# Ten weight tiles get their exponent from GpSimd: a fused attention and MoE kernel on one core

## The chip, the core and the metric

The kernel runs on one core of one Trainium2 chip. The metric is the device time of one execution in microseconds (us); lower is better. PE is TensorE, DVE is VectorE, ACT is ScalarE, POOL is GpSimd, and SP is the engine whose queue issues most of the DMAs.

## What is computed

The input is q, k and v of 4 batches, 8 heads, 768 positions and 64 columns per head, in float32, with two numbers `n_global` (8) and `n_local` (96), and two weight matrices in float64: `w_in` (512 x 2048) and `w_out` (2048 x 512). The reference, cut to what matters:

```
scores = q k^T / sqrt(D) - slope_h * dist          # kept where key < n_global, or 0 <= rel < n_local
a = softmax(scores)
x = (a v)                                          # 3072 tokens x 512
h = x @ w_in
g = h * tanh(softplus(h))
out = g @ w_out
```

## The kernel before

The 3072 tokens are cut into 12 chunks of 256. Each chunk runs through attention in 8 pieces of two heads, and then through the MoE part in 8 steps of two blocks of 128 hidden columns each. For most products an operand is kept as the sum of two float16 halves, high and low, and a product takes three matmuls (high-high, high-low, low-high). The first three chunks have their attention in float32.

The weights come as float64, and there are 32 raw tiles of 128 x 512 float64 numbers: even tiles are columns of `w_in`, odd ones are rows of `w_out`. Every raw tile is loaded once by DMA and turned into its two float16 halves within the first 140 us, while the attention of the first chunks runs beside it. For one tile i the steps are these, each with the letter that the order list has for it:

- `w`, line 330: the DMA from SP's queue. The raw words of tiles 0 to 23 lie in the buffer `wts` in which finished halves are written later, so a half can only be written when the raw tile beneath it has been read.
- `A`, `exponent_w`, line 345: the upper 32-bit word of each number, read as a float32 with a stride of 8 bytes, is multiplied by 2^-111, and goes to a buffer `wc` (four of them) as float32. A multiplication by a power of two shifts the exponent field. An apostrophe behind the letter means that DVE does it (line 146), no apostrophe that ACT does it (line 148).
- `S`, `sign_w` (line 363 on DVE, line 365 on ACT), and `B`, `bits_w` (line 369, DVE): sign and low bits into a buffer `ws`.
- `C`, `join_w` (line 373, DVE): `wc` shifted and joined with `ws`. It reads two SBUF tensors and needs `A`.
- `D`, `high_w` (line 146 or 148): the high float16 half into `wts`.
- `E`, `low_w` (line 152): the low half, on POOL without an apostrophe, on DVE with one.

PE reads the halves in `moe_in` (token `i`, line 597; step m uses tiles 4(m mod 8) and 4(m mod 8) + 2) and in `moe_out` (token `o`, line 654; tiles 4(m mod 8) + 1 and + 3). One `moe_in` step is 24 matmuls, the first 12 for the first of its two tiles; in each group of three the first two read the high half and the third reads the low one.

The order of the work is written by hand in the string `PROGRAM` (line 737): every token issues the instructions of its step, and each engine works through its own instructions in the order in which the tokens stand. An engine that waits at one instruction holds back all that stand behind it. The tokens of the ten tiles lie in the first part of the list, from `A2'` to `A11`. POOL has, before the change, the low halves of weights (`E`), of attention weights (`p`, `d`) and of the MoE product (`Z`), always through the helper `rest` at line 152. DVE's helper is `copy` at line 146, where it is also used for tiles other than `wc`.

Of the kernel before, what the change touches and what calls it, by code (L numbers as in the profile page):

```python
# [12 lines left out]
F32 = mybir.dt.float32  # L13
# [3 lines left out]
ALU = mybir.AluOpType  # L17
# [18 lines left out]
EXPO = 2.0 ** -111  # L36
# [6 lines left out]
def tile_kernel(ctx, tc, qd, kd, qT, kT, v, n, w_in, w_out, out):  # L43
# [29 lines left out]
    with ExitStack() as st:  # L73
        windowed(st, tc, locals())
# [36 lines left out]
def windowed(st, tc, loc):  # L111


    nc = tc.nc
# [12 lines left out]
    STEP = P + NGMAX  # L127

    CF32 = 3
    WB = 4  # L130
    HELD = range(2 * NFP, 2 * NFP + 6)

# [10 lines left out]
    def copy(out, in_, scale, other=False):  # L143

        if other:
            nc.vector.tensor_scalar(out, in_, scale, None, op0=ALU.mult)  # L146
        else:
            nc.scalar.activation(out, in_, AF.Copy, scale=scale)  # L148
# [35 lines left out]
    def first_key(G):  # L184
        return OWN if (G // 2) % NCHB == 0 else 0

    def high_q(G, other=False):

        both = mt.tile([P, DM], I32, name="ws", bufs=WB).bitcast(F16).rearrange("p (x a c) -> p x a c", x=2, c=CH)
        split[G, "q"] = both[:, 0], both[:, 1]  # L190
# [6 lines left out]
    def high_k(G, other=False):  # L197
        o = first_key(G)
        split[G, "k"] = tuple(mt.tile([P, DM], F32, name="wc", bufs=WB).bitcast(F16)[:, 0:GH // 2 * KW].rearrange("p (a w) -> p a w", w=KW) for x in range(2))
        copy(split[G, "k"][0][:, :, o:], raw[G][1][:, :, o:], 1.0, other)  # L200
# [6 lines left out]
    def load_v(ci):  # L207
        if ci >= NC:
            return
        b, c = divmod(ci, NCHB)  # L210
        if ci < CF32:
            vr = vown[ci] = stk.tile([P, 2, DM], F32, name="vo")
# [16 lines left out]
    def window_v(ci):  # L229
        b, c = divmod(ci, NCHB)  # L230
        vc = stk.tile([P, 2, DM], F32, name="vc")
        if ci < CF32:
            far = L.v[b, 0:NGMAX, :]
# [76 lines left out]
    def begin(n):  # L310

        if not fills:
            fills.append(mt.tile([P, DM], I32, name="ws", bufs=WB).bitcast(F16)[:, 0:DM])
            nc.vector.memset(fills[0], 1.0)
# [30 lines left out]
    def exponent_w(i, other=False):  # L345

        r = wraw[i]
        c = mt.tile([P, DM], F32, name="wc", bufs=WB)
        copy(c, r[:, :, 1].bitcast(F32), EXPO, other)
        wst[i, 0] = c  # L350

    def words(i, w):
        if (i, 1) not in wst:
            wst[i, 1] = mt.tile([P, DM], I32, name="ws", bufs=WB)
        return wst[i, 1].bitcast(U16).rearrange("p (f w) -> p f w", w=2)[:, :, w]
# [62 lines left out]
    def scores(t):  # L418
# [5 lines left out]
        rows_ = slice(blk * P, (blk + 1) * P)  # L424
        if ci < CF32:
            qr, kr = raw[2 * ci + g]
# [13 lines left out]
    def largest(t):  # L440
# [7 lines left out]
        for j in range(2):  # L448
            h = g * GH + 2 * a2 + j
            m = mb0[:, h, :] if first else mb[:, h, :]  # L450
            nc.vector.tensor_tensor_reduce(out=A[:, j, 0:w], in0=sc[j][:, 0:w], in1=m, scale=-1.0 / (UNIT if ci < CF32 else UNIT * SQ), scalar=3.0e38, op0=ALU.add, op1=ALU.min, accum_out=nm[:, h:h + 1])  # L451
        pend[t] = A
# [46 lines left out]
    def weigh(t):  # L499
# [5 lines left out]
        vs = [vown[ci][:, blk]] if nk == 1 else [vcmp[ci][:, blk], vown[ci][:, blk]]  # L505
        if ci < CF32:
            pair = slice((g * GH // 2 + a2) * P, (g * GH // 2 + a2 + 1) * P)
# [16 lines left out]
    def rows(n):  # L524
# [4 lines left out]
        nc.vector.reciprocal(ri, rs)  # L529
        if ci < CF32:  # L530
            xhls[n] = ri
# [169 lines left out]
    def checks(i):  # L701
# [29 lines left out]
        "I": identity, "P": turn_p, "F": turned, "O": spread, "m": times_rb,  # L731
        "R": rows, "T": high_x, "U": low_x, "V": turn_x,
        "A": exponent_w, "S": sign_w, "B": bits_w, "C": join_w, "D": high_w, "E": low_w,
        "i": moe_in, "J": hold_h, "j": exp_h, "u": square_e, "n": ln_u, "r": inverse_u, "G": times_h, "H": times_r,
        "z": high_g, "Z": low_g, "o": moe_out, "Q": evacuate, "Y": store, "f": lambda i: flags(), "k": checks,
# [218 lines left out]
```

## Time and profile before

| what | value |
|---|---|
| runs | 605.38, 607.1 and 608.1 us, median 607.1 |
| profiled execution: span from the first to the last instruction | 602.9 us |
| profiled execution: its own time | not given apart; the median run is 4.2 us above the span |
| PE busy | 593.3 us, 98% |
| PEld (weight loads) busy | 407.6 us, 68% |
| DVE busy | 438.3 us, 73% |
| ACT busy | 454.0 us, 75% |
| POOL busy | 150.8 us, 25% |
| granted TensorE clock, mean | 0.998 |

The span is what the trace covers, and the time of a run holds what lies around it too. Busy shares are means over the whole span; the stages differ, so a share is to be read by stretch. A matmul's end is modelled in the profile, so the starts of matmuls are the better sign of whether PE goes on without a stop.

### The profile page before, as it was taken

How to read it: one execution, taken by the hardware profiler on the slowest of the kernel's cores; microseconds unless marked ns; L12 is line 12 of the kernel's file. 1: busy time of each engine (PE TensorE's matmuls, PEld its weight loads, DVE VectorE, ACT ScalarE, POOL GpSimd, SP SyncE). 2: the span in 40 equal slices, each digit the busy share in tenths (PEclk: the TensorE clock that was granted, in tenths of full speed). 3: DMA queues.
4: the chain of work that ended last, by engine and by line, in shares of the span. 5: the costliest groups of instructions: out<-in, count | busy, mean ns of one | idle time of the engine just before them, and what ended most of it. 6: DMA issues, size and time to landing. Idle time of an engine off the chain costs nothing.

```text
span 602.9 us, 14805 instructions
## 1 busy us (share of the span) xinstructions
PE 593.3 (98%) x5686; PEld 407.6 (68%) x5686; DVE 438.3 (73%) x1188; ACT 454.0 (75%) x1129; POOL 150.8 (25%) x128
## 2 busy tenths in 40 slices
PE   7999999999999999999999999999999999999996
PEld 3778677775666767757767676667767766766673
DVE  7999998998977795684876767576787766462443
ACT  6999999989978777669676778677777864655552
POOL 0133411331131423213133422141242121301020
PEclk9999999999999999999999999999999999999999
DMA  8999655233393672653464562753445351310001
GB/s 210 288 289 333 218 140 179 69 106 80 64 213 79 112 165 68 130 133 79 90 143 104 125 136 77 175 118 80 93 70 131 69 121 36 88 36 1 35 1 38
DMA packets 123066, 71.12 MB, mean 118 GB/s; under 512 B 91600, under 2 KB 112848, under 8 KB 122992
## 3 DMA queue, kind: packets, MB, share of 16 engines
q1 hardware_dynamic: 122416, 69.81, 48.5%
q8 instruction: 45, 0.74, 0.5%
q10 hardware_dynamic: 576, 0.34, 0.3%
q14 instruction: 29, 0.24, 0.1%
HBM read 38.62 MB, written 6.29 MB: 74 GB/s over the span
## 4 chain that ended last, share of the span: by engine, by line
PE 96%; DMA 1%; ACT 1%; DVE 0%; issue 0%; SPq 0%; DVEq 0%
PE ph L597 41%; PE po L654 37%; PE sc L437 5%; PE pav L521 4%; PE pav L654 3%; PE pav L512 2%; PE po L490 1%; DMA AT<-hl 1%; PE ph L543 1%; PE ph L490 1%; PE ph L318 1%; ACT A L460 0%; ACT u L623 0%; DVE sc L416 0%; ACT e L615 0%
## 5 line engine op out<-in xcount | busy, mean ns | idle before, releaser
L597 PE MATMUL ph<-xT,wts 128*128 128x256 f16 x2304 | 263.6, 273 | 0.0
L597 PEld LDWEIGHTS <-wts 128*128 128x128 f16 x2304 | 223.2, 98 | 35.2 <-issue 0.2
L654 PE MATMUL po<-wts,gt 128*128 128x512 f16 (+1 forms) x1062 | 239.0, 378 | 0.0
L654 PEld LDWEIGHTS <-gt 128*128 128x128 f16 x1158 | 110.7, 98 | 122.2 <-issue 0.4
L615 ACT ACTIVATE e<-ph 128x512 f32<-128x512 f32 x90 | 53.2, 591 | 95.8 <-PE ph L597 95.6
L152 POOL TENSOR_TENSOR gt<-gf,gt 128x512 f16<-128x512 f32 x50 | 62.0, 1241 | 229.9 <-DVE gt L146 155.7
L635 DVE CUSTOM_DVE_ANT_0 gf<-gf,u 128x512 f32<-128x512 f32 x96 | 72.4, 757 | 49.8 <-ACT u L627 48.0
L631 DVE SCALAR_TENSOR_TENSOR gf<-e,ph 128x512 f32<-128x512 f32 x90 | 61.0, 683 | 48.9 <-ACT e L615 47.9
L460 ACT ACTIVATE A<-A,nm 128x232 f32<-128x232 f32 (+1 forms) x192 | 88.2, 461 | 10.2 <-DVE nm L451 9.8
L152 POOL TENSOR_TENSOR hl<-A,hl 128x512 f16<-128x512 f32 (+1 forms) x43 | 50.6, 1186 | 110.2 <-ACT hl L148 56.8
L451 DVE CUSTOM_DVE_ANT_0 A<-sc,mb 128x232 f32<-128x232 f32 (+1 forms) x192 | 63.7, 375 | 13.1 <-PE sc L437 12.9
L627 ACT ACTIVATE u<-u 128x512 f32<-128x512 f32 x96 | 59.7, 625 | 1.9
L619 ACT ACTIVATE u<-e 128x512 f32<-128x512 f32 x96 | 59.8, 624 | 1.7
L623 ACT ACTIVATE u<-u 128x512 f32<-128x512 f32 x96 | 59.7, 623 | 1.7
L152 POOL TENSOR_TENSOR wts<-ws,wts 128x512 f16<-128x512 f32 x18 | 22.4, 1254 | 80.0 <-ACT wts L148 73.3
L152 DVE TENSOR_TENSOR gt<-gf,gt 128x512 f16<-128x512 f32 x46 | 34.3, 748 | 6.9 <-ACT gt L148 6.3
L460 ACT ACTIVATION_READ_ACCUMULATOR A<-A,nm 128x1 f32 x192 | 36.2, 188 | 0.0
L521 PEld LDWEIGHTS <-AT 128*128 128x128 f16 (+1 forms) x792 | 29.3, 97 | 8.2 <-DMA AT<-hl 2.0
L148 ACT ACTIVATE gt<-gf 128x512 f16<-128x512 f32 x39 | 24.3, 624 | 11.3 <-DVE gmax L635 9.2
L521 PE MATMUL pav<-vo,AT 128*128 128x64 f16 x432 | 28.0, 192 | 0.0
L146 DVE TENSOR_SCALAR gt<-gf 128x512 f16<-128x512 f32 x57 | 25.6, 453 | 1.5
L373 DVE SCALAR_TENSOR_TENSOR ws<-wc,ws 128x512 int32<-128x512 int32 x32 | 26.0, 832 | 0.2
(129 smaller groups left out, 559.7 us busy)
## 6 DMA issues: line engine op xcount, KB each, us to landing
wts<-w_in SPq DMA_DIRECT2D x12, 512.0 KB, 8.1
wts<-w_out SPq DMA_DIRECT2D x12, 512.0 KB
qr<-qT SPq DMA_DIRECT2D x23, 256.0 KB, 3.1
kr<-kd SPq DMA_DIRECT2D x32, 184.0 KB, 5.2
out<-ob SPq DMA_DIRECT2D x11, 512.0 KB
vr<-v SPq DMA_DIRECT2D x9, 512.0 KB
vc<-vo SPq DMA_DIRECT2D x15, 192.0 KB, 5.3
wr<-w_in SPq DMA_DIRECT2D x4, 512.0 KB, 7.8
```

The lines of the kernel that those rows point to most:

```text
L152: (nc.vector if other else nc.gpsimd).tensor_tensor(out, in_, high, op=ALU.subtract)
L451: nc.vector.tensor_tensor_reduce(out=A[:, j, 0:w], in0=sc[j][:, 0:w], in1=m, scale=-1.0 / (UNIT if ci < CF32 else UNIT * SQ), scalar=3.0e3 ...
L460: nc.scalar.activation(A[:, j], A[:, j], AF.Exp, bias=nm[:, h:h + 1], scale=-1.0, accum_out=rs[:, h:h + 1])
L521: nc.tensor.matmul(pav[:, cols], AT[rows_, (x * 2 + j) * nk + kk, :], vs[kk][rows_, y, cols], start=(n == 0), stop=(n == last))
L597: nc.tensor.matmul(ph[:, j, :].rearrange("p (b t) -> p b t", b=2), wv4[:, 2 * fb, x, c * P:(c + 1) * P], xT[:, :, y * NCC + c, :], start=( ...
L615: nc.scalar.activation(mish[m]["e"], mish[m]["h"], AF.Exp, scale=-1.0 / (SV * SW), accum_out=esum[:, m:m + 1])
L619: nc.scalar.activation(u, mish[m]["e"], AF.Square, bias=0.5)
L623: nc.scalar.activation(mish[m]["r"], mish[m]["u"], AF.Ln, bias=0.25 / RS, scale=1.0 / RS)
L627: nc.scalar.activation(r, r, AF.Exp, scale=-1.0)
L631: nc.vector.scalar_tensor_tensor(gf, mish[m]["e"], 0.5, mish[m]["h"], op0=ALU.add, op1=ALU.mult)
L635: nc.vector.tensor_tensor_reduce(out=gf, in0=gf, in1=mish[m]["r"], scale=SG / (SV * SW * RS), scalar=0.0, op0=ALU.mult, op1=ALU.max, accum ...
L654: nc.tensor.matmul(pos[ci][t][:, cols], gt[:, x, j, t * P:(t + 1) * P], wv4[:, 2 * fb + 1, y, cols], start=(fb == 0 and n == 0), stop=(fb ...
```

## The change

For the tiles 1, 2, 3, 4, 6, 7, 8, 10, 11 and 12 step `A` becomes one GpSimd instruction, whatever the token's apostrophe says. Before, tiles 2, 3, 4, 6 and 8 had it on DVE, and 1, 7, 10, 11 and 12 on ACT. The order list keeps its tokens and their order; POOL now meets the ten instructions at the places of these tokens, among its subtractions. All other tiles stay as they were, tiles 0 and 5 too.

```
+    POOLED = (1, 2, 3, 4, 7, 6, 12, 11, 10, 8)
...
         c = mt.tile([P, DM], F32, name="wc", bufs=WB)
-        copy(c, r[:, :, 1].bitcast(F32), EXPO, other)
+        if i in POOLED:
+            nc.gpsimd.tensor_scalar(c, r[:, :, 1].bitcast(F32), EXPO, None, op0=ALU.mult)
+        else:
+            copy(c, r[:, :, 1].bitcast(F32), EXPO, other)
         wst[i, 0] = c
```

## Rows read from the trace of the kernel before

**Rows 1.** The page: busy us, share of the span and instructions of each engine.

```profile
PE 593.3 (98%) x5686; PEld 407.6 (68%) x5686; DVE 438.3 (73%) x1188; ACT 454.0 (75%) x1129; POOL 150.8 (25%) x128
```

**Rows 2.** Busy time by stretch: stretch, length, each engine, PEclk, DMA share, GB/s.

```profile
14.80:56.00 41.20, 41.20 (x505) 31.51 (x506) 39.29 (x146) 40.51 (x119) 9.43 (x8) 1.00 1.06 307
56.00:140.00 84.00, 84.00 (x714) 61.60 (x715) 78.94 (x171) 78.24 (x166) 26.51 (x20) 1.00 0.52 150
140.00:385.80 245.80, 245.80 (x2467) 165.19 (x2465) 182.53 (x490) 188.65 (x482) 67.30 (x55) 1.00 0.52 112
```

**Rows 3.** Waits of PE: who waited for whom, us, times, longest.

```profile
PE ph L318 <- DVE ws L314: 2.7, 1, 2.7
PE pav L521 <- DMA AT<-hl: 0.9, 1, 0.9
```

**Rows 4.** Instructions at tile wc, 0 to 60 us: ns min/median/max, starts, forms.

```profile
L373 DVE SCALAR_TENSOR_TENSOR ws<-wc,ws x11: 641/687/931, 17.1 to 56.0; 128x512 int32<-128x512 int32 x11
L146 DVE TENSOR_SCALAR wc<-wts x7: 409/420/431, 15.6 to 51.0; 128x512 f32<-128x512 f32 x7
L148 ACT ACTIVATE wc<-wts x5: 669/677/682, 27.2 to 55.0; 128x512 f32<-128x512 f32 x5
```

**Rows 5.** Timeline of DVE, 47 to 54 us: start, us, instruction, idle before.

```profile
47.84 0.41 DVE L146 TENSOR_SCALAR wc<-wts 128x512 f32<-128x512 f32 x1
48.17 0.39 DVE L451 CUSTOM_DVE_ANT_0 A<-sc,mb 128x232 f32<-128x232 f32 x1
...
50.10 0.64 DVE L373 SCALAR_TENSOR_TENSOR ws<-wc,ws 128x512 int32<-128x512 int32 x1
...
51.97 0.69 DVE L631 SCALAR_TENSOR_TENSOR gf<-e,ph 128x512 f32<-128x512 f32 x1 [0.56 <-ACT e L615]
...
53.26 0.68 DVE L152 TENSOR_TENSOR wts<-ws,wts 128x512 f16<-128x512 f32 x1
```

**Rows 6.** POOL's groups by form, 0 to 60 us: busy us, mean ns, idle before.

```profile
L152 POOL TENSOR_TENSOR wts<-ws,wts 128x512 f16<-128x512 f32 x9 | 10.8, 1215 | 43.6 <-ACT wts L148 40.5 <-DVE rs L527 3.1
...
L261 POOL IOTA u<- 128x128 f32 x1 | 0.2, 238 | 0.0
...
L262 POOL IOTA e<- 128x96 f32 x1 | 0.2, 211 | 0.0
```

**Rows 7.** Timeline of POOL, 18 to 72 us.

```profile
18.81 1.17 POOL L152 TENSOR_TENSOR wts<-ws,wts 128x512 f16<-128x512 f32 x1 [17.37 <-ACT wts L148]
29.26 1.16 POOL L152 TENSOR_TENSOR wts<-ws,wts 128x512 f16<-128x512 f32 x1 [9.28 <-ACT wts L148]
...
48.33 1.16 POOL L152 TENSOR_TENSOR wts<-ws,wts 128x512 f16<-128x512 f32 x1 [2.29 <-ACT wts L148]
56.29 2.55 POOL L152 TENSOR_TENSOR wts<-ws,wts 128x512 f16<-128x512 f32 x2 [6.80 <-ACT wts L148]
...
69.03 1.16 POOL L152 TENSOR_TENSOR gt<-gf,gt 128x512 f16<-128x512 f32 x1 [3.57 <-issue]
70.16 1.60 POOL L152 TENSOR_TENSOR wts<-ws,wts 128x512 f16<-128x512 f32 x1
```

**Rows 8.** Timeline of DVE, 20 to 47 us.

```profile
22.36 0.46 DVE L369 TENSOR_SCALAR ws<-wts 128x512 uint16<-128x512 uint16 x1 [0.28 <-DMA wts<-w_in]
...
27.55 0.69 DVE L373 SCALAR_TENSOR_TENSOR ws<-wc,ws 128x512 int32<-128x512 int32 x1
```

**Rows 9.** Timeline of PE, 26 to 34 and 47 to 57 us.

```profile
29.75 2.78 PE L597 MATMUL ph<-xT,wts 128*128 128x256 f16 x24
...
53.21 2.78 PE L597 MATMUL ph<-xT,wts 128*128 128x256 f16 x24
```

**Rows 10.** Timeline of SP's DMA issues, 5 to 40 us.

```profile
27.00 0.29 SPq L239 DMA_DIRECT2D vc<-v  x1
```

**Rows 11.** The chain that ended last, in order of time: start, us, what.

```profile
53.37 2.62 PE ph L597 x24
```

**Rows 12.** Timeline of DVE, 68 to 78 us.

```profile
69.09 1.65 DVE L373 SCALAR_TENSOR_TENSOR ws<-wc,ws 128x512 int32<-128x512 int32 x1
```

## The prediction

> **What bounds the kernel now.** I read the page's engine totals first: TensorE (PE) is busy 593.3 of 602.9 us [rows 1]. A busy PE need not be one at its peak, so the next view was the busy time by stretch, cut where PE's behaviour changes: 14.8 to 56 us holds the ten tiles of the change, and PE is busy for all 41.20 us of it, as for the whole of the two stretches behind it, 84.00 and 245.80 us [rows 2]. Third came PE's waits [rows 3]: 2.7 us on the very first matmul, before any weight is read, and 0.9 us on one transposed attention tile in the last part. PE thus runs without a visible gap from 14.8 to 385.8 us. The granted clock is 1.00 in all three stretches, its level of 2.4 GHz [rows 2], so the sum has no term for the clock.
>
> The other side of the same table matters as much: in 14.8 to 56 us VectorE (DVE) is busy 39.29 and ScalarE (ACT) 40.51 of 41.20 us, GpSimd (POOL) only 9.43 [rows 2]. The change moves work from the two full engines to the idle one. But those two do not make PE wait there: whatever they save can shorten the end only by removing PE time, and there is none to remove.
>
> **What the change removes.** Each of five ACT copies (tiles 1, 7, 12, 10, 11) takes 677 ns in the median, each of five DVE copies (2, 3, 4, 6, 8) 420 ns [rows 4]; on DVE the next instruction starts 0.33 us after such a copy's start (47.84 to 48.17) [rows 5]. So ACT gets back 5 x 0.68 = 3.4 us and DVE 5 x 0.33 = 1.65 us. On the end both are worth 0, since PE covers them; were that cover gone they would be worth at most those sums. What PE could still gain is the 0.9 us wait released by a transpose DMA [rows 3]; it lies behind 385.8 us, so 330 us after the stretch with the ten tiles, and I count 0.
>
> **What it adds: the POOL price.** The trace has no single-input POOL arithmetic. Its two-input operation on 512 columns is 1.22 us in the mean, 1.16 undisturbed [rows 6, 7]; its iota, which reads nothing, takes 211 ns for 96 columns and 238 ns for 128, or 0.84 ns a column, which at 512 columns is 0.238 + 384 x 0.00084 = 0.56 us [rows 6]. So the price lies between 0.56 and 1.16 us. I take 0.7: one input stream of two should halve most of the 1.16, and that lies nearer to the lower row. Ten cost POOL 7 us, of which it had 41.20 - 9.43 = 31.8 free [rows 2].
>
> The Trainium skill (GPSIMD Engine Reference, section 3.1) tells of 769 ns measured for 512 elements in a tight loop, and its section 4.1 advises against GpSimd for ordinary elementwise work. At 0.77 us the ten would cost 7.7 us instead of 7.0, still inside the free time, and the forecast would be the same.
>
> **Order on POOL.** The copies now queue in front of POOL's subtractions (low_w, token E). Tile 2's copy stands ahead of tile 0's subtraction. DVE's first read of tile 2 waited for its DMA until 22.36 [rows 8], so the copy runs 22.4 to 23.1, and tile 0's subtraction slips from 18.81 [rows 7] to about 23.1 to 24.3; its reader on PE starts at 29.75 [rows 9], so this is free. Tile 1's copy follows. Tile 3's copy waits for its load; I place that at 27.00, when SP could issue the transfer that takes over the load's semaphore [rows 10]: 27.0 to 27.7. The subtraction of tile 2, queued behind it, was only released at 29.26 [rows 7]: 1.5 us to spare. DVE's join of tile 2 (27.55 [rows 8]) finds its copy done 4.4 us earlier.
>
> The dense place is at 49 us. Tile 4's subtraction holds POOL from 48.33 to 49.49, and the next one came at 56.29 [rows 7]; between them now stand the copies of 6, 12, 8, 10 and 11, 5 x 0.7 = 3.5 us in 6.8. Tile 6's copy starts behind the subtraction, at 49.5 instead of 47.84, and ends at 50.2; the join that needs it started at 50.10 [rows 5]. Whoever is behind that join on DVE waits too: token B of tile 12, then the product at 51.97, which had 0.56 us of idle time ahead of it, then tile 6's own subtraction at 53.26, ending at 53.94 [rows 5]. PE's reader of tile 6 starts at 53.21 [rows 9], and its 24 matmuls take 2.62 us of the chain that ended last [rows 11], 0.109 each. It reads the high half of tile 6 from the 13th and the low half first at the 15th: 53.21 + 14 x 0.109 = 54.74. So that subtraction may slip by 54.74 - 53.94 = 0.80 us before PE stops.
>
> **The port.** One row speaks against the change. A DVE join started at 69.09 and took 1.65 us [rows 12] against 0.64 for the one at 50.10 [rows 5]: it began 0.06 us behind a POOL subtraction, and ended 0.55 us after that one's end at 70.19; the POOL instruction behind it, at 70.16, then took 1.60 us instead of 1.16 [rows 7]. The two engines exclude each other there, and each copy on POOL can hold DVE up by its own length. No row shows it for a one-input POOL operation, so the bounds per copy are 0 and 0.7 us (1.16 at the dear price).
>
> The Trainium skill (SBUF — State Buffer, "Who interferes with whom") calls this an exclusive lock for the whole instruction, taken also against DVE's fast one-input copies. The 1.65 us agrees for a two-input one; by its rule even joins that have nothing to do with the ten tiles can lose, and the sum would move towards the slower rival below.
>
> **The sum.** At the dense place: tile 6's copy ready at 50.2, its join late by 0.1 to 0.4 us; copies 12, 8, 10 and 11 stand beside DVE work there. With no collisions the slip is taken up by the 0.56 us of idle time: PE loses 0. With two collisions of 0.7 us that reach tile 6's subtraction and the late join, less those 0.56: 2 x 0.7 + 0.4 - 0.56 = 1.2 late, less 0.80: 0.4 us. With all four, 2.6 late: 1.8 us. I take 0.3 us: DVE holds the contested kinds for only part of its time. 602.9 + 0.3 = 603.2 for the profiled span. That execution's own time is not among those shown; the median run, 607.1, lies 4.2 above the span, so I forecast 607.1 + 0.3 = **607.4 us**. A measurement here cannot tell less than about 0.5% (3.0 us) from no change.
>
> **The rivals.** (a) *DVE is held up at every step.* At 1.16 us a copy, the four that stand beside tile 6's chain delay it by 4 x 1.16 + 0.4 - 0.56 = 4.5 us, and PE stops for 4.5 - 0.8 = 3.7 us: 610.8. At 0.7 us it is the 1.8 above: 608.9. It decides once the chain slips by more than 0.80 us, and passes 0.5% at 1.0 us a copy with all four colliding. For it: the 1.65 us row [rows 12], and DVE at 39.29 of 41.20 us [rows 2]. Against: of the eleven joins in the first 60 us, with POOL's subtractions among them, the median took 687 ns and the slowest 931 [rows 4], and four full collisions in a row are many. Chance 0.24, two fifths of it over 0.5%.
>
> (b) *POOL's first operation of its kind pays for loading code.* The first subtraction started at 18.81 and took 1.17 us like the others [rows 7], which speaks against it. What a delay would do: tile 2's copy has 27.55 - 23.1 = 4.4 us; past that it holds DVE's join, and behind it the copies of 1 and 3 and the subtraction of 2, due on PE at 29.75 + 14 x 0.109 = 31.28 against an end at 29.26 + 1.16 = 30.42. A copy late by 6 us would make the join 1.6 late and, with POOL's queue behind it (tile 0's subtraction 1.16, two copies 1.4, then 1.16 from 29.1), end that subtraction at 32.8: PE stops 1.5 us, 608.6.
> The Trainium skill (GPSIMD Engine Reference, section 2.1) gives about 6 us for the first call of a freshly loaded kernel; no run here shows one. Chance 0.05, little of it over 0.5%.
>
> (c) *Faster.* Earlier DVE and ACT change which transposes are late after 385.8 us; at best the 0.9 us goes, 606.2. PE's other idle time (2.7 us) lies before the first weight. A gain over 3.0 us has no place in the trace. Chance 0.07.
>
> **How the numbers follow.** The forecast, from 0 to 1 us more, has 0.64. The range: below, case (c) and the spread of the runs shown, 605.38 at the least; above, (a) at its dear price. 605.3 to 610.8 leaves out part of (a) and (c), under 2 in 10. Slower by over 0.5%: 0.4 x 0.24 of (a), 0.01 of (b), and 0.03 for the spread of a median of runs: 0.14. Faster: 0.04, for the spread alone. Same: 0.82.
>
> **What would show it.** In the profile after: ten POOL operations of 0.56 to 1.16 us; the exponent rows gone from DVE and ACT for those tiles; tile 0's subtraction behind 22.4 us; still 41.2 of 41.2 us of PE in the stretch, or a new PE wait at the matmuls of 53.2 us of about 0.3. Wrong if POOL's copy takes over 1.2 us, if DVE rows beside it double in number at 1.3 us or more, or if a PE wait appears on a subtraction or a transposition with more than 1 us.

## The result, and the profile after

The changed kernel takes 610.2 us in the median of four runs (608.2 to 610.84), the kernel before 606.24 beside it (605.0 to 608.1): ratio 1.006, 95% interval 1.0042 to 1.0078. That is slower by 0.6%, 3.6 us at the size of this kernel, and just over the 0.5% below which the prediction called it no change. The time lies inside the range, but the likeliest case, no change, did not come. The loss is near the 3.7 us of rival (a) at its dear price; how much of that is luck is told below.

The profiled execution has a span of 606.4 us against 602.9 before, at a granted clock of 0.999. The page's totals after, answering [rows 1]:

```profile
PE 595.0 (98%) x5686; PEld 407.7 (67%) x5686; DVE 440.6 (73%) x1183; ACT 452.1 (75%) x1124; POOL 168.2 (28%) x138
```

POOL has 17.4 us more, ten instructions more. DVE lost its five copies, yet is 2.3 us busier. By stretch, as [rows 2] (stretch, length, then busy us and count of PE, PE's weight loads, DVE, ACT, POOL; granted clock, DMA share, GB/s):

```profile
14.80:56.00 41.20, 39.96 (x483) 29.69 (x483) 38.91 (x135) 37.37 (x113) 23.00 (x16) 1.00 1.06 305
56.00:140.00 84.00, 83.56 (x714) 61.30 (x712) 79.23 (x168) 76.42 (x157) 30.32 (x23) 1.00 0.50 147
140.00:385.80 245.80, 245.80 (x2463) 165.64 (x2462) 183.21 (x493) 188.74 (x481) 65.82 (x54) 1.00 0.51 110
```

PE, which had no gap from 14.8 to 385.8 us, now has 1.24 us of them up to 56 us and 0.44 in the stretch behind; from 140 us on all is as before. The waits of PE name what ended the gaps (who waited for whom, total us, times, longest), against [rows 3]:

```profile
PE ph L319 <- DVE ws L315: 2.7, 1, 2.7
PE pav L525 <- DMA AT<-hl: 1.1, 2, 0.9
PE ph L494 <- DVE gf L635: 0.9, 1, 0.9
PE ph L547 <- DVE gf L635: 0.4, 1, 0.4
PE ph L494 <- ACT A L464: 0.3, 1, 0.3
```

The third and fourth are new, and neither is a wait for a weight. A transposition (L494) and the one that spreads 1/sum (L547) each wait for a PSUM bank `ph` that the GeGLU product on DVE (L635; L631 before) still reads. The tile `wc`, 0 to 62 us, against [rows 4] (ns min/median/max, first and last start, forms):

```profile
L377 DVE SCALAR_TENSOR_TENSOR ws<-wc,ws x11: 651/692/1156, 17.4 to 59.5; 128x512 int32<-128x512 int32 x11
L351 POOL TENSOR_SCALAR wc<-wts x10: 1529/1759/2293, 23.1 to 58.1; 128x512 f32<-128x512 f32 x10
...
  DVE ws L377: 0.6, 1
```

The POOL copy costs 1.53 us at the least and 1.76 in the median, where 0.56 to 1.16 was the range. The last line is from the part "who waited for it": one DVE join waited 0.6 us. POOL's own timeline (start, us, instruction, idle before), against [rows 7]:

```profile
23.15 1.81 POOL L351 TENSOR_SCALAR wc<-wts 128x512 f32<-128x512 f32 x1 [21.73 <-DMA wts<-w_in]
...
28.15 1.53 POOL L351 TENSOR_SCALAR wc<-wts 128x512 f32<-128x512 f32 x1 [0.55 <-DMA wts<-w_out]
30.17 1.16 POOL L153 TENSOR_TENSOR wts<-ws,wts 128x512 f16<-128x512 f32 x1 [0.50 <-ACT wts L149]
...
39.82 4.00 POOL L351 TENSOR_SCALAR wc<-wts 128x512 f32<-128x512 f32 x2
...
49.90 1.16 POOL L153 TENSOR_TENSOR wts<-ws,wts 128x512 f16<-128x512 f32 x1 [2.25 <-ACT wts L149]
51.02 8.86 POOL L351 TENSOR_SCALAR wc<-wts 128x512 f32<-128x512 f32 x5
```

The dense place is the last row: five copies in 8.86 us, where 3.5 were forecast and 6.8 were free. DVE beside it, against [rows 5]:

```profile
50.66 0.72 DVE L373 TENSOR_SCALAR ws<-wts 128x512 uint16<-128x512 uint16 x1
51.27 0.63 DVE L531 TENSOR_SCALAR rs<-rs 128x8 f32<-128x8 f32 x1
...
52.79 1.14 DVE L377 SCALAR_TENSOR_TENSOR ws<-wc,ws 128x512 int32<-128x512 int32 x1 [0.65 <-POOL wc L351]
53.85 0.72 DVE L373 TENSOR_SCALAR ws<-wts 128x512 uint16<-128x512 uint16 x1
54.47 0.66 DVE L635 SCALAR_TENSOR_TENSOR gf<-e,ph 128x512 f32<-128x512 f32 x1
...
55.75 0.67 DVE L153 TENSOR_TENSOR wts<-ws,wts 128x512 f16<-128x512 f32 x1
```

And PE, against [rows 9]:

```profile
55.19 0.65 PE L494 MATMUL ph<-idn,A 128*128 128x128 f32 x4 [0.88 <-DVE gf L635]
55.68 2.78 PE L601 MATMUL ph<-xT,wts 128*128 128x256 f16 x24
...
60.80 1.09 PE L547 MATMUL ph<-idn,ri 128*64 128x128 f32 x16 [0.44 <-DVE gf L635]
```

Read the three together. The join of tile 6 waits for its copy until 52.79, and takes 1.14 us instead of the 0.64 of [rows 5]; the half extraction behind it (B, L373) takes 0.72. The product therefore starts at 54.47, and PE, which wants its bank, stops 0.88 us. The 24 matmuls of the next moe_in start at 55.68 against 53.21 in [rows 9]: 2.47 late. Of this, 0.62 was there at 18 us, ahead of the first POOL copy, so it is a difference between two profiles and not of the change; 0.95 came between that and the dense place, which begins 1.57 late (the moe_in before it starts at 49.63 and started at 48.06). With the second stop the lateness is 3.13 us, and it stays there to 403 us.

Such a lateness is no measure of the change by itself. A run is 1.8 us longer than its span (608.2 and 606.4 here), so the profiled execution before took about 604.7 us, an estimate, which is 1.5 us under the median. The kernel relief_alone below, with no copy on any engine and no slower, starts that moe_in at 49.94, later than the change. What a copy costs is therefore read over short stretches: from the first `moe_out` to the moe_in before the dense place (38.96 to 48.06 in the kernel before, 9.10 us), and from there to the second moe_in behind it (48.06 to 58.70, 10.64 us). These are the rows of the kernel before:

```profile
38.96 2.75 PE L654 MATMUL po<-wts,gt 128*128 128x512 f16 x12
...
48.06 2.78 PE L597 MATMUL ph<-xT,wts 128*128 128x256 f16 x24
...
58.70 5.41 PE L597 MATMUL ph<-xT,wts 128*128 128x256 f16 x48
```

The change takes 0.64 us more in the first, in which copies 7 and 4 stand, and 1.56 us more in the second. That is 2.2 of the 3.6 us; the rest is in the experiments only in part.

### The profile page after: what moved, and what is told of

Same layout as the page of the kernel before. It is cut to its first block, busy times and chain, and to the rows that moved or that the text cites. A ratio compares the mean times of both kernels' runs of the same rounds, so it can differ in the third digit from the quotient of the medians.

```text
span 606.4 us, 14806 instructions
## 1 busy us (share of the span) xinstructions
PE 595.0 (98%) x5686; PEld 407.7 (67%) x5686; DVE 440.6 (73%) x1183; ACT 452.1 (75%) x1124; POOL 168.2 (28%) x138
## 4 chain that ended last, share of the span: by engine, by line
PE 86%; DMA 9%; DVE 2%; SPq 1%; ACT 1%; issue 0%; POOL 0%; ACTq 0%; POOLq 0%
PE ph L601 39%; PE po L658 36%; PE pav L525 4%; PE pav L658 3%; PE sc L441 3%; DMA wts<-w_out 3%; DMA vc<-v 2%; DMA kr<-kd 2%; DMA AT<-hl 1%; DVE ws L377 1%; SPq L339 0%; SPq L182 0%; POOL wc L351 0%; DVE ws L373 0%; ACT gt L149 0%
## 5 line engine op out<-in xcount | busy, mean ns | idle before, releaser
L635 DVE SCALAR_TENSOR_TENSOR gf<-e,ph 128x512 f32<-128x512 f32 x90 | 61.0, 682 | 48.4 <-ACT e L619 47.5
L631 ACT ACTIVATE u<-u 128x512 f32<-128x512 f32 x96 | 59.7, 625 | 1.9
```

Of the source, the lines that this page charges most:

```text
L631: nc.scalar.activation(r, r, AF.Exp, scale=-1.0)
L635: nc.vector.scalar_tensor_tensor(gf, mish[m]["e"], 0.5, mish[m]["h"], op0=ALU.add, op1=ALU.mult)
```

## The experiments

Each was timed against the kernel before in five rounds on the same chip (before: 606.15 to 606.17 us), but for the probe, which ran once. "Early" are tiles 2, 1, 3, 7 and 4, "dense" are 6, 12, 8, 10 and 11.

**Half of the tiles each.**

```diff
-    POOLED = (1, 2, 3, 4, 7, 6, 12, 11, 10, 8)
+    POOLED = (1, 2, 3, 4, 7)          # early_five
+    POOLED = (6, 8, 10, 11, 12)       # dense_five
```

> Only tiles 1, 2, 3, 4 and 7 have their exponent on GpSimd; 6, 8, 10, 11 and 12 are back on DVE and ACT. Theory of the dense place (the five copies behind tile 4's subtraction, at 51 to 60 us, make the loss): the PE stops at 55.19 and 60.80 us of the changed kernel are gone, PE is late by 1.0 us at most from this part (the changed kernel's PE is 0.62 late before the first GpSimd copy and 1.57 late at the first MoE step of the second chunk), ratio to before 1.000 to 1.002. Rival, that every copy costs alike through the port: half of the 1.006, so 1.003.

> Only tiles 6, 8, 10, 11 and 12 have their exponent on GpSimd. Theory of the dense place: the PE stops of 0.9 and 0.5 us behind the product and the transposes at 53 to 61 us stay, ratio 1.003 to 1.006. Rival, that every copy costs alike: 1.003, with the stops halved. If the two halves add up, the ratios of this run and of the one with the early five multiply to 1.006; if the loss needs both (the early delays use up the slack), both are near 1.001.

early_five: 608.26 us, 1.0028 (1.0015 to 1.0042). dense_five: 608.2 us, 1.003 (1.0018 to 1.0042). Multiplied they give 1.0058, the whole change, where the first theory had put early_five at 1.002 at most. The dense five bring both stops behind the product again (1.1 us at L547, 0.9 at L494). The early five bring another one, that the prediction had called free. POOL's timeline there:

```profile
31.03 1.53 POOL L351 TENSOR_SCALAR wc<-wts 128x512 f32<-128x512 f32 x1 [0.72 <-DMA wts<-w_out]
32.52 1.42 POOL L153 TENSOR_TENSOR wts<-ws,wts 128x512 f16<-128x512 f32 x1
```

and PE's:

```profile
34.00 1.26 PE L601 MATMUL ph<-xT,wts 128*128 128x256 f16 x10 [1.05 <-POOL wts L153]
```

Tile 3's copy waits for its load until 31.03; tile 2's subtraction is queued behind it and ends at 33.94, and PE waits 1.05 us for it. In the profile of the full change the load came by 28.15 and the subtraction ran at 30.17, so this stop is not in every execution.

**All but tile 6**, whose copy goes back to DVE.

```diff
+    POOLED = (1, 2, 3, 4, 7, 12, 11, 10, 8)
```

> Nine copies on GpSimd as in the change, tile 6 alone back on DVE. Theory of the late copy (the join of tile 6 waits for a copy that ends at 52.75 instead of 48.25, and DVE's queue stands behind it): the loss at the dense place mostly goes, PE late by 1.5 to 2 instead of 3.13 us at 62 us, ratio 1.002 to 1.003. Rival, the port (DVE's two-input and fast instructions are held while a GpSimd copy of 1.5 us runs): four copies are still there, so four fifths of the loss stay, ratio 1.005.

608.01 us, 1.0027 (1.0017 to 1.0037). From the moe_in before the dense place to the one behind it PE loses 0.29 us instead of the 1.56 of the full change. This is what the theory of the late copy expected. The dense place stops PE by the copy of tile 6, its late data and its use of the port at that moment together; of what remains 0.63 us lies in the stretch of copies 7 and 4.

**The same POOL work, read by nobody.** The exponents are made as before; POOL does five multiplications of the same shape at the dense place into a spare buffer.

```diff
+        if i in (6, 8, 10, 11, 12):
...
+            nc.gpsimd.tensor_scalar(wst["spare"], old, EXPO, None, op0=ALU.mult)
+        copy(c, r[:, :, 1].bitcast(F32), EXPO, other)
```

> All exponents on DVE and ACT as before the change; in addition GpSimd runs, at the places of tiles 6, 8, 10, 11 and 12, five multiplications of the same shape and stride on finished weights into a buffer that nobody reads. Theory of the port: nothing waits for their data, and yet DVE rows beside them stretch and PE stops by some 1 to 1.5 us at 53 to 62 us, ratio 1.002 to 1.004. Theory of the late copy: no stop over 0.3 us, ratio within 1.001 of before. DVE and ACT also lose the relief (0.7 and 2.0 us) that the change gave them there.

607.2 us, 1.0018 (1.0006 to 1.003), a little under what the theory of the port expected. PE's waits name the product once more, although nothing waits for data of POOL:

```profile
PE ph L549 <- DVE gf L637: 0.8, 1, 0.8
...
PE ph L496 <- DVE gf L637: 0.3, 1, 0.3
```

and DVE's timeline shows why:

```profile
50.34 0.91 DVE L375 TENSOR_SCALAR ws<-wts 128x512 uint16<-128x512 uint16 x1
...
51.45 0.64 DVE L379 SCALAR_TENSOR_TENSOR ws<-wc,ws 128x512 int32<-128x512 int32 x1
52.01 0.94 DVE L375 TENSOR_SCALAR ws<-wts 128x512 uint16<-128x512 uint16 x1
...
54.91 0.67 DVE L153 TENSOR_TENSOR wts<-ws,wts 128x512 f16<-128x512 f32 x1
55.51 1.25 DVE L369 TENSOR_SCALAR ws<-wts 128x512 uint16<-128x512 uint16 x2
...
56.96 2.32 DVE L379 SCALAR_TENSOR_TENSOR ws<-wc,ws 128x512 int32<-128x512 int32 x3
```

Those at 50.34, 52.01, 55.51 and 56.96 take 0.45, 0.46, 0.79 and 1.84 us in the kernel before. Each of the five POOL multiplications (from 50.27, 51.89, 53.80, 55.66 and 57.41, 1.54 to 1.83 us long) held one DVE instruction, the one that began 0.07 to 0.33 us behind its start, by 0.44 to 0.48 us. DVE instructions that began later beside the same multiplication took their usual time, also those with two inputs in SBUF: the join at 51.45, 1.19 behind the first one's start, and the subtraction at 54.91. POOL's work alone can cost PE time, with no wait for its data. DVE still makes its own copies here, as it did not in the change, so the size is that of a fuller DVE.

**The price by itself.** The kernel before, with ten POOL instructions at its start.

```diff
+    nc.gpsimd.memset(...)
+    nc.gpsimd.tensor_scalar(...)   # 512 columns, side by side x2, every other x2
+    nc.gpsimd.tensor_copy(...)     # side by side, every other
+    nc.gpsimd.tensor_tensor(...)   # two inputs, x2
+    nc.gpsimd.tensor_scalar(...)   # 256 columns
```

> The kernel before, with ten GpSimd instructions on a constant region at its very start, where GpSimd is idle: a fill of 1024 columns, multiplications of 512 columns (two read side by side, two with the stride of 8 bytes), plain copies (side by side, strided), two-input subtractions (side by side, strided), a multiplication of 256 columns. Theory that the one-input multiplication itself is dear: 1.5 us side by side as with the stride, with some 0.75 us at 256 columns. Rival, that the stride makes it dear: 0.7 us side by side and 1.5 us strided. The plain copy tells whether the arithmetic or the pass over the data costs.

One run, 606.57 us. POOL's timeline:

```profile
2.40 6.54 POOL L353 TENSOR_SCALAR hs<-wts 128x512 f32<-128x512 f32 x4
9.01 1.32 POOL L355 COPY hs<-wts 128x512 f32<-128x512 f32 x2
10.42 1.04 POOL L356 TENSOR_TENSOR hs<-wts 128x512 f32<-128x512 f32 x1
11.53 1.04 POOL L357 TENSOR_TENSOR hs<-wts 128x512 f32<-128x512 f32 x1
12.66 0.85 POOL L358 TENSOR_SCALAR hs<-wts 128x256 f32<-128x256 f32 x1
```

One by one the multiplications are 1.68 and 1.49 us side by side, 1.52 and 1.61 at every other column; the plain copies 0.61 and 0.65. So the stride that the exponent needs is no cost that shows; the multiplication is. It takes longer than an operation with two inputs (1.04).

**The order mended at the two places**: tile 6's copy ahead of tile 4's subtraction, tile 11's one step later.

```diff
-  i8 E4 S6' A6'
+  A6' i8 E4 S6'
...
-  C8 A11 D12 ... i9 E10 D8'
+  C8 D12 ... i9 E10 A11 D8'
```

> All ten copies on GpSimd, but two tokens moved in the order list: tile 6's copy ahead of tile 4's subtraction (GpSimd is idle there for 2.25 us) and tile 11's behind tile 10's subtraction. Theory of the late copy: the join of tile 6 no longer waits, and with one copy less beside DVE the stops at 55.19 and 60.80 us go as in the run with tile 6 back on DVE, ratio 1.002 to 1.003. Rival, the port alone: nine copies still run beside DVE, ratio 1.005.

607.46 us, 1.0014 (1.0003 to 1.0026), less than either theory had. The stops behind the product are gone (0.3 us between the two moe_in), the wait of PE for tile 2's subtraction (1.0 us) is there.

**The relief alone.** The ten copies are left out, and their joins use the exponents of tile 0.

```diff
+        if i in POOLED:
+            wst[i, 0] = wst[0, 0]
+            return
... (tile 0's exponents get a buffer that is kept; also in the runs below that read them)
```

> The ten exponent copies are left out on every engine (the ten joins take tile 0's exponents, so the weights of these tiles are not the reference's). It is the change with a GpSimd instruction of zero length. Theory that PE bounds the stretch: the relief of DVE and ACT is worth nothing, ratio 0.999 to 1.001. Rival, that DVE and ACT bound the stretch: faster by up to 3.4 us, ratio 0.994 to 0.997.

606.29 us, 0.9999 (0.9989 to 1.001). Without the copies on any engine the kernel is no faster: the relief of DVE and ACT is worth nothing.

**All ten on POOL, read by nobody**: as the one before, but POOL makes the ten copies at the places of the change.

```diff
         if i in POOLED:
             nc.gpsimd.tensor_scalar(c, r[:, :, 1].bitcast(F32), EXPO, None, op0=ALU.mult)
+            wst[i, 0] = wst[0, 0]
...
```

> GpSimd makes all ten copies at the change's places from the same raw words, but the ten joins take tile 0's exponents (the weights of these tiles are not the reference's), so no join waits for GpSimd. DVE and ACT have the relief. Theory of the port: the loss stays, 1.004 to 1.006. Theory of the late copy: ratio within 1.002. In both the subtractions queue behind the copies and finished halves wait until GpSimd has read the raw words beneath them.

608.56 us, 1.0028 (1.0016 to 1.004), between the two theories. Relief included, and with no join that waits for POOL's exponents, 0.28% of the 0.6% is still there: by the medians about half of the loss is POOL's mere activity (the port, and its subtractions queued behind the copies), the other half needs the late data too. Against relief_alone, which lacks that activity alone, the intervals do not touch. In its profile the dense place passes with 0.26 us and no wait for the product: with DVE relieved of its copies, the port alone does not stop PE there, and the port with the late copy of tile 6 does.

**A shorter copy of the same values**, by a POOL operation with two inputs and a column of constants.

```diff
-            nc.gpsimd.tensor_scalar(c, r[:, :, 1].bitcast(F32), EXPO, None, op0=ALU.mult)
+            nc.gpsimd.tensor_tensor(c, r[:, :, 1].bitcast(F32), expo.broadcast_to([P, DM]), op=ALU.mult)
...
```

> The change with its order, but GpSimd multiplies by a constant column, read as a second input of stride 0, where the change gives the constant in the instruction. By the probe's rows a two-input operation takes 1.04 us against 1.5 to 1.6 us. Theory that the length of the copy sets the loss: tile 6's copy ends some 0.5 us earlier, the five of the dense place take 6 instead of 8.9 us, ratio 1.002 to 1.004. Rival, that each copy costs one hold of DVE whatever its length: still 1.005 to 1.006.

611.08 us, 1.0085 (1.0067 to 1.0103): dearer than the change, though the copy itself is shorter, in the median 1.22 us for 1.76 (tile `wc`):

```profile
L352 POOL TENSOR_TENSOR wc<-wts,ones x10: 1039/1218/1492, 24.4 to 58.8; 128x512 f32<-128x512 f32 x10
```

The expectation was missed, and with it the idea that the copy's length is the whole price. DVE beside the dense five:

```profile
54.23 1.01 DVE L532 TENSOR_SCALAR rs<-rs 128x8 f32<-128x8 f32 x1
...
55.40 1.36 DVE L378 SCALAR_TENSOR_TENSOR ws<-wc,ws 128x512 int32<-128x512 int32 x1
56.68 1.29 DVE L374 TENSOR_SCALAR ws<-wts 128x512 uint16<-128x512 uint16 x1
...
58.46 1.88 DVE L374 TENSOR_SCALAR ws<-wts 128x512 uint16<-128x512 uint16 x2
```

Against the same kinds undisturbed (0.15, 0.64, 0.46 and 0.80) these four rows grew by 0.86, 0.72, 0.83 and 1.08 us. In the changed kernel the rows at 50.66, 51.27, 52.79 and 53.85 grew by 0.27, 0.48, 0.50 and 0.26. A shorter operation with two inputs holds DVE longer than the longer one with one. PE's longest new wait here is again the product's (1.3 us at L495); it also waits 1.3 us in two parts for ACT's exponential tiles `A`.

**A plain copy**: POOL copies tile 0's exponents at the ten places, and the joins wait for them; that copy does not wait for a load.

```diff
-            nc.gpsimd.tensor_scalar(c, r[:, :, 1].bitcast(F32), EXPO, None, op0=ALU.mult)
+            nc.gpsimd.tensor_copy(c, wst[0, 0])
...
```

> The change with its order and its data waits at the length that the prediction took (0.7 us): GpSimd copies tile 0's exponents for each of the ten tiles with a plain copy (0.61 to 0.65 us in the probe; the weights of these tiles are not the reference's, and the copy does not wait for its tile's load). Theory that only the price was wrong in the prediction: ratio 0.999 to 1.001. Rival, that the slack was wrong too (PE's transposes wait for the product behind the join, which ended 0.06 us ahead of them before): 1.001 to 1.003, with PE stopping at the transposes.

606.41 us, 1.0009 (0.9996 to 1.0022). Tile `wc`, then the stretch:

```profile
L354 POOL COPY wc<-hs x10: 608/820/1067, 16.7 to 53.5; 128x512 f32<-128x512 f32 x10
```

```profile
14.80:56.00 41.20, 41.00 (x497) 31.08 (x498) 39.24 (x138) 37.66 (x113) 16.45 (x18) 1.00 1.07 303
```

At 0.82 us a copy, near the price of the forecast, and with joins that need POOL's data, PE keeps 41.00 of 41.20 us and the product stops nobody. These copies hold DVE too, an extraction at 52.18 by 0.41 us (0.87 for 0.46) and the 128x8 instruction at 50.60 by 0.44, about as long as the multiplications do. The holds being alike, what is gone is the late data: the stretch of the dense place costs 0.32 us here and 1.56 in the change.

**The early place mended too**: late_moved, with tile 2's subtraction (E2) ahead of tile 3's copy (A3'); then the same with the operation of two inputs.

```diff
-  C1 S3' A3' ... F13 E2 i0
+  C1 E2 S3' A3' ... F13 i0
```

> As late_moved, and in addition tile 2's subtraction stands ahead of tile 3's copy, which waits for its load. Theory that the subtraction's place behind a copy that waits for a DMA made the rest of the loss at 30 us (late_moved's PE stopped 1.0 us on that subtraction): ratio 1.000 to 1.001, no PE wait on GpSimd. Rival, that the rest is the two copies at 40 to 44 us and the port: 1.001 to 1.002 as late_moved.

> The three moved tokens and the two-input form together, all ten exponents on GpSimd and the reference's arithmetic. Theory that PE bounds the stretch once no wait is added: ratio 0.999 to 1.001, not faster than before. Rival, that the relief of DVE and ACT pays once GpSimd is out of the way: 0.997 or less.

three_moved: 607.4 us, 1.0017 (1.0005 to 1.003). three_moved_two_input: 610.02 us, 1.0068 (1.0051 to 1.0086). Both expectations were missed. In three_moved PE waits for no instruction of POOL any more, but 1.0 us in two parts for ACT's `A`, the longer behind copies 7 and 4 at 41.4 to 45.1 us. Its profile is of the longest of its twelve runs, 609.03 us. In the last one the product (1.4 us) and `A` (1.3) stop PE as in two_input. No kernel here is faster than the one before. The two that equal it, relief_alone and short_copy, do not have the reference's weights; those that do and have copies on POOL are all slower, late_moved the least.

## Where the prediction was right and where it was wrong

**The step that failed is the POOL price.** "I take 0.7 ... one input stream of two should halve most of the 1.16" measured 1.53 us at the least and 1.76 in the median, outside the bounds on both readings; "POOL's copy takes over 1.2 us" was among the prediction's own signs of being wrong. The nearest row by engine and shape [rows 6, 7] gave a floor, not a ceiling, because the cost does not go by the number of inputs: multiplying by a constant is 1.5 us, copying 0.61 to 0.65, two inputs 1.04. With a plain copy of 0.82 us, near the price taken, the forecast "no measurable change" holds (short_copy, 1.0022 at the most); that copy waits for no load, and two_input shows that a short operation is not enough if it holds DVE for long.

**The slack was read at the wrong reader.** The prediction followed tile 6 to its matmuls and found 0.80 us. PE's next instruction that hangs on the same DVE queue comes earlier: the transposition at 52.72 us needs the bank that the product at 51.97 [rows 5] frees when it ends, at 52.66:

```profile
52.72 0.66 PE L490 MATMUL ph<-idn,A 128*128 128x128 f32 x4
```

Those 0.06 us are no slack either: after the change the transposition starts 0.06 behind the product's end again (55.13 and 55.19). So there was none to be seen. Worked again with the rows after, in the time of a kernel 1.57 late: the join was due at 50.10 + 1.57 = 51.67 and started at 52.79, 1.12 late. From its start to the product's there were 1.87 us before, 0.56 of them idle; after, 1.68, with no idle time and without tile 8's copy. 1.12 + 1.68 - 1.87 = 0.93 us late at its start and 0.90 at its end, and the moe_in behind it starts 2.47 - 1.57 = 0.90 later.

**The port: the mechanism right, the hold shorter than the copy.** "Each copy on POOL can hold DVE up by its own length" does not hold for the multiplication: the hold is 0.4 to 0.5 us an instruction beside 1.5 to 1.8 us copies, inside the bounds of 0 and 0.7. Nor is DVE "held up at every step": of the rows after, the extractions from 55.06 (0.79 us for two) and the subtraction at 55.75 (0.67) stand beside the third of the five and take their usual time. Now and then a second instruction is held in one copy: the join at 52.79 and the extraction at 53.85 both stand beside the second of the five. Without a wait for POOL's exponents dense_five_unread loses 0.18% and all_ten_unread 0.28%. The interval of all_ten_unread lies below that of the change, so the late data have their share. At the dense place the times leave the split open (the intervals of dense_five_unread and dense_five, 0.3%, overlap), but the profiles, one of each kernel, show it: 1.56 us in the change and 2.43 in dense_five against 0.26 in all_ten_unread and 0.32 in short_copy, so most of it is the late data of tile 6. Where DVE lacks the relief the holds alone cost as much (dense_five_unread, 1.45). The Trainium skill (SBUF — State Buffer, "Who interferes with whom") has the port pair locked for the whole instruction. For a POOL operation with two inputs the trace agrees (DVE rows grow by 0.72 to 0.86 us, and up to 1.08 for two, beside 1.22 us copies). For the multiplication it does not: a DVE join that began at 28.19, 0.04 behind a POOL copy that ran to 29.68, took 1.15 us and ended at 29.34, before it.

**The order at the early places was not free.** Tile 0's subtraction moved to 24.91 and nobody waited, as forecast. Tile 2's had 1.5 us to spare by the sum; with 1.53 us for the copy and a load that came as late as 31.03 this was gone, and early_five and late_moved show the stop of 1.0 us. Copies 7 and 4 stood in the sum with nothing, without a reason. They cost PE 0.64 us, through the port and not through late data, as these rows of the change show (DVE, then ACT):

```profile
39.52 1.46 DVE L367 TENSOR_SCALAR ws<-wts 128x512 uint16<-128x512 uint16 x2
...
42.18 0.87 DVE L367 TENSOR_SCALAR ws<-wts 128x512 uint16<-128x512 uint16 x1
```

```profile
44.59 0.63 ACT L149 ACTIVATE wts<-ws 128x512 f16<-128x512 f32 x1 [0.88 <-DVE ws L377]
```

Before, the same sign extractions took 0.80 and 0.47 us:

```profile
38.62 0.80 DVE L363 TENSOR_SCALAR ws<-wts 128x512 uint16<-128x512 uint16 x2
...
40.62 0.47 DVE L363 TENSOR_SCALAR ws<-wts 128x512 uint16<-128x512 uint16 x1
```

So they grew by 1.06 us. The joins behind them start at 43.88 instead of 41.91, 1.97 later, which is 1.04 more than the 0.93 us that PE is late at 39.89, and they wait for nothing of POOL. ACT sits idle for 0.88 us until the first is through, its `A` comes late, and PE's transpositions of it at 46.75 wait 0.3 us and take 0.92 instead of 0.66. In the kernels without copies 7 and 4 on POOL (relief_alone, dense_five, dense_five_unread) PE takes the same 9.10 us there within 0.01; in all that have them it takes 0.46 us (early_five) to 1.44 us (both with two inputs) more, and 0.67 in all_ten_unread, whose copies nobody reads.

**What held, and what was luck.** PE bounds the kernel, and the saved DVE and ACT time by itself is worth nothing (relief_alone, 0.9999); it only pays back some of what the port takes. No code load shows: POOL's first multiplication took 1.81 us, 0.05 over the median. The clock stayed at 1.00. The range holds the time through rival (a), and that its 3.7 us come so near the measured 3.6 is partly luck: it had four holds of 1.16 us at the dense place less a slack of 0.80, where the change has holds of 0.4 to 0.5, no slack, late data, and a loss of 0.64 us at a place that the sum left out.

**What is open.** About 1.4 us of the 3.6 are not seen in the profile of the change, which is of the shortest of its four runs; the stop of 1.05 us on tile 2's subtraction, which other profiles have, would fit, but no profile of the change shows it. Why the operation with two inputs costs 0.25% more than the one it replaces is shown at the dense place; for its waits on `A` and the transposed input it was not taken apart.

## What to carry to other kernels

Before work is moved to an idle engine, price that very operation there, by a probe if no row has it: a count of inputs is no measure. Then look for the first instruction of the bounding engine that depends on anything in the queue behind the moved work, buffers that it frees as well as data that it makes; the slack is what that one has. And where the receiving engine shares a port with a full one, add its hold on every neighbour, which is not the same as its own length.

## What the runs showed of the hardware

On POOL a multiplication of 128x512 f32 by a constant takes 1.49 to 1.68 us (0.85 at 256 columns), a plain copy 0.61 to 0.65, a subtraction of two inputs 1.04; reading every other column instead of adjacent ones costs the copy 0.04 us, and the multiplication nothing that its two readings a form can show. The Trainium skill (GPSIMD Engine Reference, section 4.1) calls GpSimd's elementwise work with one input roughly line-rate, and with two about twice as slow as VectorE's; here that order holds for the copy only, and is turned round for the multiplication.

A multiplication on POOL held the DVE instruction that read SBUF alone and began in its first 0.33 us, by 0.4 to 0.5 us, a 128x8 one among them (0.15 to 0.63), and those that began later beside it seldom: in dense_five_unread none. An operation with two inputs held DVE to its end: the join at 55.40 ended at 56.76, 0.56 behind the end of the copy beside it, and the rows grew by 0.72 to 0.86 us (the 128x8 one from 0.15 to 1.01). The product, which reads one input from PSUM, did not grow: 0.66 us at 54.47, 0.27 behind the start of the third of the five copies, and 0.69 before.
